# A fifth score buffer, batch 0's routing behind the score loop, expert 0 begun on half its slots, and a low half moved in the ramp

## The chip, the cores and the metric

One core of one Trainium2 chip runs the whole program. The metric is the device time of one execution in microseconds. Five engines work side by side, each on its own instruction stream in its own order: TensorE (PE, matrix products), VectorE (DVE), ScalarE (ACT), GpSimd (POOL) and SyncE (SP, which here only issues DMA transfers, one after the other). They are kept in step by semaphores that the framework sets from the tiles that instructions read and write.

## The reference

Three layers follow each other. Attention has 2 batches of 8 heads, 768 positions and 64 channels; a query sees only the keys whose 6 sign bits (of the product with a random projection) equal its own:

```python
mask = q_bucket[:, :, :, None] == k_bucket[:, :, None, :]
scores = np.where(mask, scale * np.matmul(q, k.transpose(0, 1, 3, 2)), -1000000000.0)
scores = scores - np.max(scores, axis=-1, keepdims=True)
attn = np.exp(scores); attn = attn / (np.sum(attn, axis=-1, keepdims=True) + 1e-09)
x = np.matmul(attn, v)                              # -> 1536 tokens of 512 channels
```

A mixture of 8 experts follows: the softmax of `x @ w_gate` picks one expert for each token and a weight for it; each expert takes at most 384 tokens, in order, and the rest give zero:

```python
h = np.maximum(np.einsum('ecd,edf->ecf', disp, w1), 0.0)   # 512 -> 1024
y = np.einsum('ecf,efd->ecd', h, w2)                       # 1024 -> 512
out[i] = gate_w[i] * y[expert_idx[i], pos[i]]
```

Last is a dense layer, 512 to 2048 to 512: `h = x @ w_in; g = h * np.clip(h + 3.0, 0.0, 6.0) / 6.0; g @ w_out`.

## The kernel before

**Numbers in two halves.** Products that need more precision than one 16-bit pass are made of a high half (a rounded copy) and a low half (what the rounding left). So a value x appears as `hi` and `lo`, `phi` and `plo`, `wh` and `wl`, `xh` and `xl`, `hh` and `hl`; the high half is a copy by ACT or DVE, the low half a subtraction by DVE or POOL, and PE makes three products: high by high, high by low, low by high.

**The score loop.** The 16 heads have 6 blocks of 128 keys each, 96 blocks in all, and `for k in range(STEPS + LAG + 2)` runs over them in steps. In step k the program order is: work that is due by k - 0.5; `high(k-1)`, the cast `phi` of the exponentials `pf` (ACT, or DVE where `on_dve` says so); `scores(k)`, four matmuls and two exponentials by ACT into a tile `pf` (a ring of four buffers with the tag `pf`); `low(k-2)`, the subtraction `plo = pf - phi` (POOL, except that DVE does all but two of the last twelve); `mx(k+8)`, two matmuls into a ring of three PSUM buffers, each followed by a maximum on DVE (the row maxima must be known before a head's scores); at odd k `pv` of two older blocks (36 matmuls); and work that is due by k. Work is put down in a table `later` by `at`, `spread` and `stages` with a step as its time; the table `Q` holds most of these steps. Each engine then executes its own part strictly in this order. `on_dve` reads `Q["hl"]` for the last twelve steps, counted from step 84.

**The operands of a head.** Before a head's maxima can be computed, its q and k must stand in the four tiles X, Y, K1, K2 of `sets[h % 4]`, as high and low halves beside rows of sign bits. `halves` allots the tiles `hi` and `lo` (from head 2 on one buffer each, which the heads use in turn). For head 3 and later, `prep(h)` lets ACT make `hi`, then issues on SP two transfers of sign bits (`put_bits`) and four of `hi` into the set; its second part makes `lo` (DVE, `low_half`, one `scalar_tensor_tensor`) and sends it with two transfers (`send_low`). For head 3 the two parts are due at steps 6 and 7.25. Heads 0 to 2 go through `prep0`: ACT writes the high halves straight into the set, and only `lo` is sent by DMA. In `prep0` the low half of heads 0 and 1 is made by POOL out of a scaled copy `rs`, that of head 2 by DVE, both its parts at step 5 (`at(5.0, run, pre[2])`).

A buffer that is written again must have been read to the end by everything that used it: the `lo` of head 3 goes into the buffer from which the `lo` of head 2 is sent.

**The end of the loop and the transition.** `route(b)` works out, for the tokens of batch b, the expert and the place among its slots (`oh`, `rh`, and `ohr`, six columns of one-hot rows); `weigh(b)` works out the gate's weight (`jg`, `j`, `rg`). For batch 0 both are spread over the last steps of the loop, mostly on DVE. `evac(h)` divides a head's sums by the row sums (three DVE operations that read PSUM; `xp`); for head 14 it is due at step 93.5, for head 15 it stands behind the loop (`scaled`, `columns`). Behind it comes batch 1's routing, then the one-hot products `windows` that give `ids` and `gates`, the gather of expert 0's tokens from memory, their scaling, transposition (`psa`) and split into `xh` and `xl`. `heat(n)` issues n matmuls whose result nobody reads. `high_w` casts a 512-column piece of a weight (ACT), `low_w` makes the low halves of pieces that are cast (DVE), in order, and the number of them that it makes at a call depends on how many are there.

**The experts.** Each expert has 224 slots in two groups of `GW` = 112. `gemm1(e, f)` makes 128 of the 1024 hidden channels: 12 matmuls of 224 columns into one of three PSUM buffers `psh`, then ACT writes `hh` and DVE `hl` from it. `gemm2` follows, then the dense layer, whose output is scattered to memory.

Of the kernel before, what the change touches and what calls it, by code (L numbers as in the profile page):

```python
# [63 lines left out]
def moe_attention_kernel(ctx, tc, qk, v, vt, pj, wg, w1, w2, win, wout, out, cap):  # L64
# [212 lines left out]
    def weigh(b):
# [33 lines left out]
    Q = {'tk': (84, 86), 'v': (-3.25, -4.75, -1.75, -2.25), 'vg': (-6.5, -6.75), 'vgd': 1, 'pr': (-13.0, -12.75, -12.0, -12.5), 'prd': 0.6, 'b0': 7.75, 'b': 1.75, 'bd': 0.5, 'vm0': (9.5, 10.5, 11.5, 12.5), 'vm': (-0.5, 4.75, 7.0, 12.25), 'vs': 13.25, 'pa': 1.5, 'ev': 0.5, 'lvt': -5.0, 'v4': (2.0, 4.25, 10.0, 16.25), 'vg0': (1.85, -4.4, 9.0), 'p2': 3.5, 'lr': (0.25, 1.25, 2.25), 'lv': 4.0, 'vsd': 0.75, 'ac': (1, 1, 2, 4, 6, 7, 8, 10), 'hd': (3, 5, 17), 'hn': (0, 0, 3, 1, 1, 1, 0, 0), 'ap': (0,), 'h0': (7,), 'hl': (6,), 'l0': (), 'll': (1, 3), 'ht': (6, 3, 7, 6, 3, 2)}  # L311
# [4 lines left out]
    with ExitStack() as actx:  # L316
# [346 lines left out]
        def unmatched(r):  # L663
# [10 lines left out]
            m = pt.tile([P, S], F32, tag="pf", name=f"um{r}", bufs=4)  # L674
# [12 lines left out]
            y = pt.tile([P, S], F32, tag="pf", name=f"uy{r}", bufs=4).rearrange("p (c h d) -> p c h d", c=NC, h=2)  # L687
# [33 lines left out]
        def vsplit(h):  # L721
# [17 lines left out]
            if h > 3:  # L739
# [4 lines left out]
        fill = pt.tile([P, S], F32, tag="pf", name="fill", bufs=4)  # L744
# [107 lines left out]
        at(5.0, run, pre[2])  # L852
# [38 lines left out]
        at(STEPS - 2, store, NH // 2 - 1, 0, D)  # L891
# [697 lines left out]
```

## Time and profile before

| | |
|---|---|
| runs | 652.09, 653.40, 652.09 us; median 652.09 |
| the profiled execution | 653.98 us, of which its span is 652.3 us |
| PE busy | 623.4 us (96%), 5530 instructions |
| DVE busy | 478.8 us (73%), 1056 |
| ACT busy | 435.9 us (67%), 882 |
| POOL busy | 234.0 us (36%), 222 |
| score loop | to 218.6 us |
| transition | 218.6 to 232.8 us |
| experts, dense layer, scatter | from 232.8 us |

The span is the time from the first instruction to the last; 1.7 us of the execution lie outside it. All times below are microseconds from the span's start. In a timeline a row is a group of like instructions without a gap: start, length, engine, line of the kernel, operation, result<-operands, how many; in square brackets the engine's idle time just before and what ended it. "DVE L459" there is an instruction of line 459 of the kernel above. In a table of windows each engine has its busy time in the stretch and the number of instructions; PEclk is the clock that TensorE was granted, as a share of the full one.

### The profile page before, as it was taken

The numbers are of one execution on the slowest core, as the hardware profiler recorded it, in microseconds if no ns is written. First come the engines' busy times: TensorE is split into PE (matmuls) and PEld (weight loads), VectorE is DVE, ScalarE is ACT, GpSimd is POOL, SyncE is SP. The second block draws the span as 40 slices with busy tenths as digits, with TensorE's granted clock in tenths as the row PEclk, the third lists the DMA queues.
The fourth block names the chain that finished last, engine by engine and source line by source line (L and its number), as shares of the span: only waits on it lengthen the run. The fifth ranks groups of instructions, "written<-read, shape, count | busy, mean of one in ns | idle before, by whom it ended". The sixth has DMA issues, their size and how long they took to land.

```text
span 652.3 us, 14467 instructions
## 1 busy us (share of the span) xinstructions
PE 623.4 (96%) x5530; PEld 452.5 (69%) x5530; DVE 478.8 (73%) x1056; ACT 435.9 (67%) x882; POOL 234.0 (36%) x222
## 2 busy tenths in 40 slices
PE   8999999999998799999999999999999999999892
PEld 3678788788887589999999985555555555555441
DVE  6889998898999888888988887888887332222410
ACT  8878888788888657677777745554445685555820
POOL 6666978978994142210866100000000020000021
PEclk9999999999999999999999999999999999999997
DMA  6658568656474188877677553444440020000011
GB/s 196 204 137 230 166 159 230 167 132 179 100 203 145 36 286 276 250 248 238 207 241 252 164 170 117 135 129 140 151 131 31 1 81 17 1 1 0 2 50 53
DMA packets 35732, 92.19 MB, mean 141 GB/s; under 512 B 6778, under 2 KB 12250, under 8 KB 35650
## 3 DMA queue, kind: packets, MB, share of 16 engines
q1 hardware_dynamic: 32562, 83.75, 43.2%
q0 software_dynamic: 2400, 7.36, 3.4%
q8 instruction: 46, 0.75, 0.5%
q14 instruction: 36, 0.29, 0.1%
q10 hardware_dynamic: 688, 0.03, 0.1%
HBM read 67.14 MB, written 6.29 MB: 113 GB/s over the span
## 4 chain that ended last, share of the span: by engine, by line
PE 56%; DMA 4%; ACT 3%; issue 1%; DVE 1%; POOL 0%; POOLq 0%; DVEq 0%; ACTq 0%
PE psg L1363 17%; PE pso L1390 15%; PE psy L1141 11%; PE psh L1114 11%; DMA out_dram<-os,inv 3%; ACT junk L1317 2%; PE psa L1091 1%; ACT gh L1373 1%; DVE rl L1366 1%; DMA xg<-xd,ids 1%; DMA xd<-xp 1%; ACT rl L1365 0%; POOL xg L1072 0%; ACT xp L944 0%; POOL out_dram L1405 0%
## 5 line engine op out<-in xcount | busy, mean ns | idle before, releaser
L493 POOL TENSOR_TENSOR plo<-pf,phi 128x768 f16<-128x768 f32 x86 | 145.3, 1713 | 19.7 <-DVE phi L489 10.0
L1405 POOL DMA_INDIRECT out_dram<-os,inv x12 | 12.1, 1012 | 272.6 <-DVE os L1397 244.5
L482 ACT ACTIVATE pf<-pst 128x384 f32<-128x384 f32 x192 | 83.1, 486 | 30.0 <-PE pst L481 25.3
L459 DVE TENSOR_REDUCE mx<-psm 128x1 f32<-128x384 f32 x192 | 96.0, 546 | 6.8 <-PE psm L456 6.6
L164 DVE SCALAR_TENSOR_TENSOR wl<-raw,wh 128x1024 f16<-128x1024 f32 (+1 forms) x68 | 83.4, 1230 | 5.8 <-ACT wh L158 5.1
L1363 PE MATMUL psg<-yTh,ch 128*128 128x512 f16 (+1 forms) x256 | 83.4, 326 | 3.2 <-DVE rl L1366 3.2
L1363 PE MATMUL psg<-yTl,ch 128*128 128x512 f16 (+1 forms) x256 | 83.4, 326 | 0.0
L1363 PE MATMUL psg<-yTh,cl 128*128 128x512 f16 (+1 forms) x256 | 83.4, 326 | 0.0
L1366 DVE SCALAR_TENSOR_TENSOR rl<-rl,psg 128x512 f32<-128x512 f32 x64 | 35.0, 551 | 64.4 <-ACT rl L1365 64.0
L480 PE MATMUL pst<-Y,K 128*128 128x384 f32 x192 | 74.9, 390 | 2.5 <-ACT pf L482 2.5
L1363 PEld LDWEIGHTS <-ch 128*128 128x128 f16 x512 | 50.1, 98 | 35.9
L487 ACT ACTIVATE phi<-pf 128x768 f16<-128x768 f32 x85 | 71.7, 844 | 1.9
L1390 PE MATMUL pso<-ch,gh 128*128 128x512 f16 x192 | 72.8, 379 | 0.0
L1390 PE MATMUL pso<-ch,gl 128*128 128x512 f16 x192 | 72.8, 379 | 0.0
L1390 PE MATMUL pso<-cl,gh 128*128 128x512 f16 x192 | 72.8, 379 | 0.0
L158 ACT ACTIVATE wh<-raw 128x1024 f16<-128x1024 f32 (+1 forms) x68 | 67.4, 998 | 0.5 <-issue 0.5
L1390 PEld LDWEIGHTS <-gh 128*128 128x128 f16 x384 | 37.6, 98 | 42.3
L1141 PE MATMUL psy<-hh,wl 128*128 128x224 f16 x256 | 66.3, 259 | 0.0
L1141 PE MATMUL psy<-hl,wh 128*128 128x224 f16 x256 | 66.3, 259 | 0.0
L1141 PE MATMUL psy<-hh,wh 128*128 128x224 f16 x256 | 66.3, 259 | 0.0
L481 PE MATMUL pst<-X,K 77*128 77x384 f32 x192 | 65.4, 341 | 0.6 <-DMA X<-rm 0.6
L508 PE MATMUL psv<-vh,phi 128*128 128x73 f16 x576 | 64.0, 197 | 0.0
(251 smaller groups left out, 1477.2 us busy)
## 6 DMA issues: line engine op xcount, KB each, us to landing
raw<-in_w_dram SPq DMA_DIRECT2D x64, 512.0 KB
rc<-in_win_dram SPq DMA_DIRECT2D x16, 512.0 KB
rc<-in_wout_dram SPq DMA_DIRECT2D x16, 512.0 KB
r<-in_qk_dram SPq DMA_DIRECT2D x16, 384.0 KB
K<-hi SPq DMA_DIRECT2D x26, 192.0 KB
vr<-in_v_dram SPq DMA_DIRECT2D x4, 768.0 KB
vt<-in_vt_dram SPq DMA_DIRECT2D x8, 384.0 KB
K<-lo SPq DMA_DIRECT2D x16, 192.0 KB
```

The lines of the kernel that those rows point to most:

```text
L158: act.activation(wh[e, i][:, c : c + n], r, AF.Copy, scale=(S1, S2)[i // 2])
L164: dve.scalar_tensor_tensor(out=wl[e, i][:, c : c + n], in0=r, scalar=(S1, S2)[i // 2], in1=wh[e, i][:, c : c + n], op0=ALU.mult, op1=ALU.s ...
L459: dve.tensor_reduce(out=mm[:, c, n : n + 1], in_=ps[:, :HS], axis=AX.X, op=ALU.max)
L480: pe.matmul(ps[:, :HS], st["K1"][:, kc], st["Y"][:, qc], start=True, stop=False)
L481: pe.matmul(ps[:, :HS], st["K2"][0:77, kc], st["X"][0:77, qc], start=False, stop=True)
L482: act.activation(pf[:, qc], ps[:, :HS], AF.Exp, scale=0.125 / SC / SC)
L487: act.activation(phi_t[k], pf_t[k], AF.Copy)
L493: eng.tensor_tensor(out=plo_t[k], in0=pf_t.pop(k), in1=phi_t[k], op=ALU.subtract)
L1114: pe.matmul(ps, l[:, c], r[:, k], start=n == 0, stop=n == 3 * KD - 1)
L1141: pe.matmul(ps, l, r, start=n == 0, stop=n == 3 * KF - 1)
L1363: pe.matmul(ps, l, x, start=n == 0, stop=n == 3 * KD - 1)
L1390: pe.matmul(po[blk][s], l, r, start=first and n == 0, stop=last and n == 2)
```

## The change

Five edits, which touch different places.

1. **The ring `pf`** has five buffers instead of four; every tile with this tag is declared so.
2. **The ramp.** The low half of head 2 is made by POOL, out of a scaled copy that POOL makes too, before the loop (one more `next(pre[2])`). Its two transfers are issued at step 6.5 instead of 5, behind the first part of `prep(3)`, which stays at step 6.
3. **The end of the loop.** `hl` goes from (6,) to (8, 10): of the last steps' casts, DVE makes `phi` 92 and 94 instead of 90. `tk` loses 86, so one small POOL copy goes; another is left out for head 15. Batch 0's `jg` and `j` operations go from DVE to POOL. Its `rg` and its six `ohr` columns come behind the loop, three of the columns by ACT (two activations each). `evac(14)` moves from step 93.5 to 97.5, the store of head 14's half from 94 to 98.
4. **Weight pieces of expert 0.** Of the five `high_w` behind the loop one stays there, one comes behind head 15's `xp`, and four (one of which stood elsewhere) come behind `run(rgen)`; the `low_w(1)` behind the loop goes, and `low_w(2)` moves behind `weigh(1)`. The pieces of low halves that are left for the first `low_w()` of the expert loop are four instead of three.
5. **Expert 0.** `begin(f, i)` issues, for f = 0 and 1, the four matmuls of the first slot group (112 columns) with `wh` (i = 0) and `wl` (i = 1). The first set stands between the two groups' transposes, the others behind the second's. `gemm1` then makes for these f the rest: `wh` by `xl` for the first group, and all three products for the second. The `heat` between the two groups (`HT[4]`) has 2 matmuls instead of 3, and the one behind them (`HT[5]`, 2 matmuls) goes.

```diff
+            if c == n - 1 if b else c < 3:
                 off = rtile([P], "off")
                 act.activation(off, iota_r, AF.Square, bias=place[:, c : c + 1], scale=-1.0)
...
         def prep0(h):
             r, hi, lo = halves(h)
+            x = pt.tile([P, S], F32, tag="pf", name=f"rs{h}", bufs=5)
             if h < 2:
                 act.activation(x, r, AF.Copy, scale=SC)
+            else:
+                pool.tensor_scalar(out=x, in0=r, scalar1=SC, scalar2=None, op0=ALU.mult)
...
-            if h < 2:
-                pool.tensor_tensor(out=lo, in0=x, in1=f32(hi), op=ALU.subtract)
-            else:
-                low_half(lo, r, hi)
+            pool.tensor_tensor(out=lo, in0=x, in1=f32(hi), op=ALU.subtract)
             yield
             send_low(h, lo)
...
         run(pre[1])
+        next(pre[2])
         load_r(4)
...
-        at(5.0, run, pre[2])
+        at(6.5, run, pre[2])
...
-                at(k + Q["ev"], evac, h)
+                at(k + Q["ev"] if h < NH - 2 else 97.5, evac, h)
...
+        r0, w0 = route(0, lambda: misc("psr0")), weigh(0)
+        stages(r0, [66 + 1.5 * i for i in range(8)] + [84.5, 85.25, 87.25, 87.75, 88.25])
+        stages(w0, (84, 86, 87.25, 88.5, 90.5, 91.5))
...
-        for q in range(4):
-            high_w(wp1, 0, 0, 512 * q, 512)
-        high_w(wp1, 0, 1, 0, 512)
-        low_w(1)
+        run(w0)
+        high_w(wp1, 0, 0, 0, 512)
+        run(r0)
         heat(ps_t, "t", HT[0])
...
+    def begin(f, i):
+        if i == 0:
+            begun[f] = ps_h.tile([P, W], F32, tag="h", name=f"psh0{f}")
+        l = (wh, wl)[i][0, 0]
+        for k in range(KD):
+            c = slice(k * 512 + f * P, k * 512 + (f + 1) * P)
+            pe.matmul(
+                begun[f][:, 0:GW], l[:, c], xs_t[0][0][:, k, 0:GW], start=i + k == 0, stop=False, skip_group_check=True
+            )
...
+        todo = [(l, r, 0, W) for l, r in ((a, xh), (b, xh), (a, xl))]
...
+            todo = [(a, xl, 0, GW)] + [(l, r, GW, W) for l, r in ((a, xh), (b, xh), (a, xl))]
...
     run(rgen)
+    for q in range(2, 4):
+        high_w(wp1, 0, 0, 512 * q, 512)
+    for q in range(2):
+        high_w(wp1, 0, 1, 512 * q, 512)
...
-    low_w(2)
     run(wgen)
     windows(ps2, ohr, rg, [B - 1])
     heat(HT[3])
+    low_w(2)
...
     low_w(1)
+    begin(0, 0)
     scale_x(0, 1)
     lows.append(make_x(0, 1))
-    heat(HT[5])
+    begin(0, 1)
+    begin(1, 0)
+    begin(1, 1)
```

What SP issues in the ramp, before (`lo2`, `hi3` and `lo3` are the halves of heads 2 and 3, `b0` the sign bits; the number ahead of a row is its place in the engine's stream):

```order
23 L378 DMA K12_148<-lo2_252 64x768
24 L379 DMA Y2_147<-lo2_252 64x768
25 L415 DMA X3_150<-b0_302 12x768
26 L416 DMA K23_153<-b0_302 12x768
27 L403 DMA X3_150<-hi3_589 64x768
28 L404 DMA K23_153<-hi3_589 64x768
29 L405 DMA K13_152<-hi3_589 64x768
30 L406 DMA Y3_151<-hi3_589 64x768
31 L378 DMA K13_152<-lo3_591 64x768
32 L379 DMA Y3_151<-lo3_591 64x768
```

And in the changed kernel:

```order
23 L415 DMA X3_150<-b0_304 12x768
24 L416 DMA K23_153<-b0_304 12x768
25 L403 DMA X3_150<-hi3_589 64x768
26 L404 DMA K23_153<-hi3_589 64x768
27 L405 DMA K13_152<-hi3_589 64x768
28 L406 DMA Y3_151<-hi3_589 64x768
29 L379 DMA K12_148<-lo2_252 64x768
30 L380 DMA Y2_147<-lo2_252 64x768
31 L379 DMA K13_152<-lo3_591 64x768
32 L380 DMA Y3_151<-lo3_591 64x768
```

The two transfers of `lo2` go from ahead of the sign bits and of `hi3` to behind them, and are now the last ones before those of `lo3`.

What DVE does at the end of the loop, before:

```order
455 L296 TENSOR_TENSOR jg0_4355<-jg0_4355,j20_4357 128x24
456 L297 TENSOR_SCALAR j20_4357<-jg0_4355 128x6x4
457 L489 CAST phi90_4422<-pf90_4342 128x768
458 L493 TENSOR_TENSOR plo90_4424<-pf90_4342,phi90_4422 128x768
459 L273 TENSOR_SCALAR ohr_110<-iota_r_70,pl0_4271 128x128 x2
460 L204 TENSOR_TENSOR rg_109<-oh_103,j20_4357 128x384
461 L493 TENSOR_TENSOR plo91_4440<-pf91_4359,phi91_4411 128x768
462 L273 TENSOR_SCALAR ohr_110<-iota_r_70,pl0_4271 128x128
463 L518 TENSOR_SCALAR rd14_4480<-psv14_4301,sc3_3283 128x6
464 L521 RECIPROCAL rd14_4480<-rd14_4480 128x6
465 L526 TENSOR_TENSOR xp14_4479<-psv14_4301,rd14_4480 128x6x72
466 L659 CAST nflag_164<-psu_4407 1x8
```

And now:

```order
453 L661 TENSOR_REDUCE nflag_164<-nflag_164 1x1
454 L489 CAST phi92_4483<-pf92_4412 128x768
455 L493 TENSOR_TENSOR plo92_4485<-pf92_4412,phi92_4483 128x768
456 L493 TENSOR_TENSOR plo93_4496<-pf93_4423,phi93_4472 128x768
457 L489 CAST phi94_4537<-pf94_4474 128x768
458 L493 TENSOR_TENSOR plo94_4539<-pf94_4474,phi94_4537 128x768
459 L493 TENSOR_TENSOR plo95_4541<-pf95_4487,phi95_4535 128x768
460 L518 TENSOR_SCALAR rd14_4580<-psv14_4301,sc3_3285 128x6
461 L521 RECIPROCAL rd14_4580<-rd14_4580 128x6
462 L526 TENSOR_TENSOR xp14_4579<-psv14_4301,rd14_4580 128x6x72
463 L204 TENSOR_TENSOR rg_109<-oh_103,j20_4355 128x384
464 L273 TENSOR_SCALAR ohr_110<-iota_r_70,pl0_4272 128x128 x3
```

The `jg` and `j` operations and the one-hot columns are gone from between the subtractions, the cast of block 90 with them; the casts of 92 and 94 have come in, and head 14's evacuation (`rd14`, `xp14`) stands behind the last subtraction, followed by `rg` and three one-hot columns.

What DVE does between the last two gather scalings and the first `hl` of expert 0, before:

```order
588 L164 SCALAR_TENSOR_TENSOR wl0_1_4635,wlo_88<-raw0_1_0_4084,wh0_1_4634 128x512
589 L1080 TENSOR_SCALAR xg01_5152<-xg01_5152,gates_78 128x512
590 L1097 SCALAR_TENSOR_TENSOR xl0_5192<-psa00_5193,xh0_5191 128x4x112
591 L1097 SCALAR_TENSOR_TENSOR xl0_5192<-psa01_5204,xh0_5191 128x4x112
592 L164 SCALAR_TENSOR_TENSOR wl0_1_4635,wlo_88<-raw0_1_0_4084,wh0_1_4634 128x512
593 L164 SCALAR_TENSOR_TENSOR wl0_1_4635,wlo_88<-raw0_1_1_4108,wh0_1_4634 128x512 x2
594 L1118 SCALAR_TENSOR_TENSOR hl0_5230<-psh00_5231,hh0_5229 128x224
```

And now:

```order
577 L164 SCALAR_TENSOR_TENSOR wl0_0_4623,wlo_88<-raw0_0_1_4025,wh0_0_4622 128x512
578 L1082 TENSOR_SCALAR xg01_5163<-xg01_5163,gates_78 128x512
579 L1099 SCALAR_TENSOR_TENSOR xl0_5203<-psa00_5204,xh0_5202 128x4x112
580 L1099 SCALAR_TENSOR_TENSOR xl0_5203<-psa01_5219,xh0_5202 128x4x112
581 L164 SCALAR_TENSOR_TENSOR wl0_1_5151,wlo_88<-raw0_1_0_4086,wh0_1_5150 128x512 x2
582 L164 SCALAR_TENSOR_TENSOR wl0_1_5151,wlo_88<-raw0_1_1_4110,wh0_1_5150 128x512 x2
583 L1142 SCALAR_TENSOR_TENSOR hl0_5257<-psh00_5213,hh0_5256 128x224
```

Ahead of `hl0` stood three weight pieces behind the two `xl`; now four stand there.

## Rows read from the trace of the kernel before

**Rows 1.** Windows by stage: busy us per engine with instructions, clock, DMA share, GB/s.

```profile
176.00:203.00 27.00, 26.03 (x340) 21.73 (x336) 25.72 (x60) 22.10 (x42) 23.10 (x18) 1.00 0.60 166
...
203.00:219.00 16.00, 14.22 (x247) 11.65 (x247) 15.32 (x37) 13.98 (x27) 3.62 (x6) 1.00 0.36 106
...
233.00:250.00 17.00, 17.00 (x180) 16.82 (x179) 16.09 (x49) 11.70 (x31) 5.38 (x5) 1.00 0.91 306
...
644.00:652.30 8.30, 0.00 (x0) 0.00 (x0) 0.00 (x0) 0.00 (x0) 0.96 (x1) 0.50 0.09 34
```

**Rows 2.** Timeline of DVE in the ramp: start, duration, engine, line, operation, wait.

```profile
30.21 3.41 DVE L374 SCALAR_TENSOR_TENSOR lo<-r,hi 128x768 fp32r<-128x768 f32 x1
...
34.02 2.40 DVE L459 TENSOR_REDUCE mx<-psm 128x1 f32<-128x384 f32 x5
...
37.43 0.96 DVE L374 SCALAR_TENSOR_TENSOR lo<-r,hi 128x768 fp32r<-128x768 f32 x1 [1.00 <-DMA Y<-lo]
...
42.06 0.62 DVE L419 TENSOR_SCALAR b<-psb,pj_sb 128x384 fp32r<-128x384 f32 x1 [0.61 <-PE psb L430]
```

**Rows 3.** Timeline of POOL in the ramp.

```profile
29.55 3.25 POOL L493 TENSOR_TENSOR plo<-pf,phi 128x768 f16<-128x768 f32 x2
```

**Rows 4.** Timeline of SP in the ramp: its DMA issues, same columns.

```profile
33.65 0.55 SPq L378 DMA_DIRECT2D K<-lo  x1
...
36.62 0.52 SPq L403 DMA_DIRECT2D X<-hi  x1
...
40.75 0.71 SPq L379 DMA_DIRECT2D Y<-lo  x1
```

**Rows 5.** Windows at the ramp's transfers (DMA share: second number from the end).

```profile
42.00:43.00 1.00, 1.00 (x7) 0.91 (x7) 0.94 (x2) 0.39 (x1) 1.00 (x2) 1.00 1.07 267
...
43.00:44.00 1.00, 1.00 (x9) 0.34 (x9) 0.93 (x4) 1.00 (x4) 1.00 (x2) 1.00 0.64 141
...
44.00:45.00 1.00, 1.00 (x6) 0.82 (x6) 1.00 (x4) 1.00 (x3) 1.00 (x1) 1.00 0.00 0
```

**Rows 6.** Timeline of ACT in the ramp.

```profile
31.80 0.87 ACT L482 ACTIVATE pf<-pst 128x384 f32<-128x384 f32 x2 [1.61 <-PE pst L481]
...
33.66 0.84 ACT L370 ACTIVATE hi<-r 128x768 fp32r<-128x768 f32 x1 [0.98 <-DVE vh L738]
```

**Rows 7.** Timeline of PE at steps 9 and 10.

```profile
39.43 0.51 PE L456 MATMUL psm<-K,X 76*128 76x384 f32 x2
...
41.90 0.44 PE L480 MATMUL pst<-Y,K 128*128 128x384 f32 x1
```

**Rows 8.** Timeline of ACT in the loop's last fifth.

```profile
177.59 0.87 ACT L482 ACTIVATE pf<-pst 128x384 f32<-128x384 f32 x2 [1.24 <-POOL vh L741]
...
207.99 0.87 ACT L482 ACTIVATE pf<-pst 128x384 f32<-128x384 f32 x2 [1.70 <-POOL plo L493]
...
215.43 0.84 ACT L487 ACTIVATE phi<-pf 128x768 f16<-128x768 f32 x1
```

**Rows 9.** Timeline of DVE at the loop's end.

```profile
206.20 1.81 DVE L273 TENSOR_SCALAR ohr<-iota_r,pl 128x128 f16<-128x128 f16 x2
...
213.41 0.61 DVE L526 TENSOR_TENSOR xp<-psv,rd 128x432 f32<-128x432 f32 x1
...
214.20 3.67 DVE L493 TENSOR_TENSOR plo<-pf,phi 128x768 f16<-128x768 f32 x4
...
218.81 0.23 DVE L518 TENSOR_SCALAR rd<-psv,sc 128x6 f32<-128x6 f32 x1 [0.34 <-PE psv L510]
```

**Rows 10.** Timeline of POOL at the loop's end.

```profile
206.29 1.66 POOL L493 TENSOR_TENSOR plo<-pf,phi 128x768 f16<-128x768 f32 x1
```

**Rows 11.** Timeline of PE at expert 0's first gemm.

```profile
232.82 0.54 PE L1114 MATMUL psh<-xh,wh 128*128 128x224 f16 x4 [0.20 <-ACT xh L1094]
```

**Rows 12.** Timeline of DVE at expert 0's first gemm.

```profile
234.56 1.09 DVE L164 SCALAR_TENSOR_TENSOR wl<-raw,wh 128x512 f16<-128x512 f32 x1
...
235.58 0.38 DVE L1118 SCALAR_TENSOR_TENSOR hl<-psh,hh 128x224 f16<-128x224 f32 x1
```

More of the change, by code (lines that the diff above doesn't have):

```diff
@@ L267, in route @@
                 yield
-            if b and c == n - 1:
+            if c == n - 1 if b else c < 3:
                 off = rtile([P], "off")
@@ L291, in weigh @@
         jt = rtile([n, NW], f"jg{b}")
-        dve.tensor_tensor(out=jt, in0=jo[:, b], in1=bc(gt[:, b], NW), op=ALU.mult)
+        eng = dve if b else pool
+        eng.tensor_tensor(out=jt, in0=jo[:, b], in1=bc(gt[:, b], NW), op=ALU.mult)
         j2 = rtile([n, 2 * NW], f"j2{b}", F16)
-        dve.tensor_copy(j2[:, :, 0:NW], jt)
+        eng.tensor_copy(j2[:, :, 0:NW], jt)
         yield
-        dve.tensor_tensor(out=jt, in0=jt, in1=j2[:, :, 0:NW], op=ALU.subtract)
-        dve.tensor_scalar(out=j2[:, :, NW:], in0=jt, scalar1=LS, scalar2=None, op0=ALU.mult)
+        eng.tensor_tensor(out=jt, in0=jt, in1=j2[:, :, 0:NW], op=ALU.subtract)
+        eng.tensor_scalar(out=j2[:, :, NW:], in0=jt, scalar1=LS, scalar2=None, op0=ALU.mult)
         yield
@@ L366, in halves @@
             if h == 1:
-                hi = pt.tile([P, S], F32, tag="pf", name=f"hi{h}", bufs=4).bitcast(F32R)
+                hi = pt.tile([P, S], F32, tag="pf", name=f"hi{h}", bufs=5).bitcast(F32R)
             else:
@@ L673, in unmatched @@
                 sp.dma_start(out=x, in_=rows)
-            m = pt.tile([P, S], F32, tag="pf", name=f"um{r}", bufs=4)
+            m = pt.tile([P, S], F32, tag="pf", name=f"um{r}", bufs=5)
             ps = misc(f"psu{r}")
@@ L738, in vsplit @@
             dve.memset(t[:, :, DE:VA], 1.0)
-            if h > 3:
+            if 3 < h < NH - 1:
                 c = t[:, :, VA + o : VA + o + 1]
                 pool.tensor_copy(c, c)
-        fill = pt.tile([P, S], F32, tag="pf", name="fill", bufs=4)
+        fill = pt.tile([P, S], F32, tag="pf", name="fill", bufs=5)
         neg, zrow = fill[0:1], fill[32:33]
@@ L890, in moe_attention_kernel @@
             at(STEPS - 8 + i, load_w, 0, 2, i)
-        at(STEPS - 2, store, NH // 2 - 1, 0, D)
+        at(STEPS + 2, store, NH // 2 - 1, 0, D)
         def due(k):
@@ L946, in moe_attention_kernel @@
                 store(h // 2, D, P, slice(c - 2, c + 1))
+        high_w(wp1, 0, 0, 512, 512)
         rgen = route(1, lambda: misc("psr2"))
@@ L1101, in make_x @@
         return low
+    begun = {}
+    def begin(f, i):
[7 more added lines that the diff above has]
+            )
     def gemm1(e, f):
@@ L1108, in gemm1 @@
         a, b = wh[e, f // 4], wl[e, f // 4]
-        ps = ps_h.tile([P, W], F32, tag="h", name=f"psh{e}{f}")
-        n = 0
-        for l, r in ((a, xh), (b, xh), (a, xl)):
+        todo = [(l, r, 0, W) for l, r in ((a, xh), (b, xh), (a, xl))]
+        ps = None
+        if e == 0:
+            ps = begun.pop(f, None)
+        if ps is None:
+            ps = ps_h.tile([P, W], F32, tag="h", name=f"psh{e}{f}")
+        else:
+            todo = [(a, xl, 0, GW)] + [(l, r, GW, W) for l, r in ((a, xh), (b, xh), (a, xl))]
+        n = KD * len(todo)
+        for l, r, u, v in todo:
             for k in range(KD):
+                n -= 1
                 c = slice(k * 512 + (f % 4) * P, k * 512 + (f % 4 + 1) * P)
-                pe.matmul(ps, l[:, c], r[:, k], start=n == 0, stop=n == 3 * KD - 1)
-                n += 1
+                pe.matmul(
+                    ps[:, u:v], l[:, c], r[:, k, u:v], start=u == 0 and v == W and r is xh and l is a and k == 0,
+                    stop=n == 0, skip_group_check=v - u < W,
+                )
         i = e * KF + f
```

12 lines of the change are left out of this document (4 added, 8 removed).

## The prediction

> **What bounds the kernel now.** I read the windows by stage first, then the timelines at the places that the five edits touch, engine by engine, and on them only what stands in square brackets: who was waited for. In the score loop (to 218.6) two engines are nearly full. From 176 to 203 DVE is busy for 25.72 of 27 us and PE for 26.03; in the loop's last 16 us it is DVE with 15.32, against 14.22 for PE and 13.98 for ACT [rows 1]. So a wait that DVE or PE gets early in the loop is not made good later, and work taken from DVE at the loop's end is worth its own time until ACT becomes the bound. From 233 on PE is full (17.00 of 17, [rows 1]): there only matmul time and what delays the first gemms count. The transition between them is a chain (routing of batch 1, store, gather, transposes) that the change leaves in its order; it moves as a whole with the loop's end, and I cost it at 0: what is added to it (weight pieces on ACT and DVE) stands where these engines wait for the gather.
>
> **The ramp: where the change costs.** `lo` has one buffer. `lo3` is written into it by DVE and has to wait until both transfers of `lo2` have read it. Before, the trace shows this wait: `lo3` starts at 37.43 after 1.00 of idle time that ended with DMA Y<-lo [rows 2]. The first of the pair was issued at 33.65 and took 0.55 to issue [rows 4], so the second went out at about 34.2 and the pair was through 3.2 later.
>
> What the edit takes away: DVE's `lo2`, 3.41 us at 30.21, since POOL subtracted beside it (29.55, two in 3.25 [rows 3]); the same operation took 0.96 at 37.43 [rows 2]. ACT's `hi3` waited 0.98 for it [rows 6], because `lo2` reads the single `hi` buffer. That wait goes: `pf` at 31.80 ends at 32.67, `hi3` runs to about 33.5. The two POOL operations that make `lo2` instead stand ahead of the loop, where POOL waits for a scale; 0.
>
> What it adds: on SP the pair `lo2` now stands behind four transfers of `hi3`, and these can't go before `hi3` is there, at 33.5. Before, the same four and a pair behind them (that of `lo3`) were issued from 36.62 to 40.75 [rows 4], 4.13 us for the start of the last. The DMA engines were full with them (1.07 from 42 to 43, 0.64 from 43 to 44, nothing from 44 to 45 [rows 5]): data moved until about 43.6, that is 7.0 from the first issue. By this row the new pair is through at 33.5 + 7.0 = 40.5; with a notice that comes 1 later (44.6 is the latest that the empty window allows, taking the notice as up to 1 behind the data), at 41.5. The low end is 33.5 + 4.13 + 3.2 - 1.2 = 39.6: pace of the issues as before without the slowest one's excess of 1.2 over the others (estimate), and the pair's 3.2 behind its second issue. I take L = 41.2, near the row that shows six transfers in this order, against 37.43 before.
>
> The Trainium skill bears on this in "DMA: Bandwidth & Descriptors", section "Queues, rings and completion order": on each DMA engine the descriptors of one issuing sequencer's ring are consumed in the order of the ring. By that, `lo2` can't overtake `hi3`, and L would lie at the upper part of my bounds; if it could overtake, at 37 or so and no wait would be left. Rows 5 agree with a full queue, but no row shows the order inside it.
>
> Who waits for that: behind `lo3` on DVE stand the maxima of `mx(16)`; PE has three PSUM buffers for them, `mx(16)` takes two, the first of `mx(17)` the third, and the second of `mx(17)` needs the first maximum to be done. That is L + 0.96 [rows 2] + 0.48 (five maxima in 2.40 [rows 2]). Behind it in PE's order stand `pv` of two blocks and then `scores(10)`. Before, the second `mx(17)` started at about 39.6 (the pair of 39.43 [rows 7]) and `scores(10)` at 41.90 [rows 7], 2.3 later. So now `scores(10)` comes at L + 0.96 + 0.48 + 2.3 = L + 3.74 = 44.94, which is 3.04 late. With L of 39.6 it is 1.4, with 41.9 it is 3.7. Everything behind is fed by `scores`, and the one idle time of DVE that could take some of it up, 0.61 at 42.06 [rows 2], waits for PE and moves with it. The 1.0 that PE gains earlier, since the maxima come sooner, ends at this wait. Term: **+3.0** (1.4 to 3.7).
>
> **The fifth buffer.** ACT waited for POOL before it could write `pf`: 1.24 at 177.59 [rows 8] and three shorter ones between 157 and 186, 2.3 in all as the upper bound of the gain. But DVE is full in that stretch [rows 1], and ACT isn't; an ACT that runs ahead gives DVE nothing to do sooner than it can. At the least the gain is 0. I take **-0.3**, by the small gap that DVE has there.
>
> **The end of the loop.** From DVE's stream go six one-hot columns (1.81 for two at 206.20, beside POOL's subtraction at 206.29 [rows 9, 10]; the others a quarter to 0.4 each; 2.5 in all), `jg` and `j` (about 0.6), `rg` (0.5), head 14's evacuation (three operations, of which `xp` at 213.41 is the longest, 0.61 [rows 9]; 1.0) and a cast (0.6): 5.2. Two casts come in, 1.1. DVE alone would end its last subtraction 4.1 sooner than at 217.87 (four of them in 3.67 from 214.20 [rows 9]), at 213.8. ACT sets a limit close by: its last cast began at 215.43 and lasted 0.84; its wait of 1.70 for POOL at 207.99 [rows 8] goes with the fifth buffer, and one cast of 0.75 goes to DVE, so it ends at 216.27 - 1.70 - 0.75 = 213.8. The last subtraction (0.92) is behind that cast: 214.8, or up to 215.5 if POOL's subtraction slows DVE elsewhere as it did at 206.20. Before, `scaled` of head 15 began at 218.81 [rows 9], 0.94 after the last subtraction, for the last `pv`. Now DVE has 1.0 for the evacuation, 0.5 for `rg` and three columns (0.6) in front of it: 2.1, longer than `pv`. So `scaled` is at 216.9 to 217.6. Term: **-1.4** (-1.0 to -1.9): of the 4.1 us moved, DVE's new tail and ACT keep the rest.
>
> **Expert 0.** Four matmuls of 224 columns took 0.54 at 232.82 [rows 11], of which ends overlap; over the stretch it is 180 matmuls in 17.00 us [rows 1], 0.094 each. Behind the last `xh` PE has for f = 0 and 1 32 matmuls of 112 columns, at half of that 1.5, instead of 24 with 2.3: about -0.7. But DVE has four weight pieces ahead of `hl0` instead of three. A piece takes 0.61, and 1.09 at 234.56 beside POOL; `hl0` ran at 235.58 [rows 12], 2.8 after the first gemm's start. PE has three `psh` buffers, so f = 3 waits for `hl0`, which comes 0.6 later against a PE that is 0.7 ahead, and f = 4 for `hl1`, with a larger piece between. PE therefore stops where it did not before (17.00 of 17 [rows 1]). Bounds: -0.7 (nothing waits) and +0.7 (a piece at 1.09 and one more behind it). I take **+0.4**, by the row at 234.56, where two such pieces stood already.
>
> **Sum.** 3.0 - 0.3 - 1.4 + 0.4 = +1.7. The profiled execution took 653.98, span 652.3 and 1.7 around it, and lies 1.89 above the median 652.09. So 655.7 for an execution like that one, and 653.8 for the median.
>
> **Rivals.**
> *The transfers are not late.* If the DMA engines take the six faster when nothing else is queued and the pair is through by 37.5, 4 us from the first issue, `lo3` waits no longer than before, and DVE and ACT keep the 1.0 that they gain from the missing `lo2`. The point from which it decides is L = 41.90 - 3.74 = 38.2: below that the ramp gains. For it: the lone pair needed 3.2. Against it: six transfers in a full queue needed 7.0 [rows 4, 5]. Time: -0.3 - 1.4 + 0.4 - 0.5 = -1.8, 650.3: faster.
> *The wait is short, or the later terms are larger.* L at 39.6 (+1.4), or the fifth buffer worth 1.5 instead of 0.3: the sum is about 0, 652.1. For it: bounds above; against it: the full DMA windows and the full DVE.
> *The clock falls.* In the new gap PE has little to do from about 38.4 to 43, which before it never had in the loop. After the last matmul the granted clock is 0.50 [rows 1], the lower of the two levels (1.2 GHz). If that happens in the gap, some 3 us of PE work behind it take twice as long, of which the idle shares around it take half: +1.5, 655.3. Against it: the gap is short beside the 8 us of that row. The Trainium skill ("TensorE: Matmul & The Clock Gate", section "What's actually happening") says that an idle engine goes to half the clock and returns after sustained work; by it this rival would hold if the gap were long enough, and the trace shows only the end of the program.
>
> **How the numbers follow.** Forecast 0.46 (its own range 652.7 to 655.0), clock 0.12, short wait 0.20, transfers not late 0.22. A measurement tells 0.2%, 1.3 us, from no change: 650.8 and 653.4 are the marks. Of the forecast three quarters lie above 653.4 (0.34) and the clock's 0.12 with it: slower 0.46. The short wait gives 0.18 and the forecast's lower part 0.12 to the same: 0.30. The rest, 0.24, is faster. The range goes from 650.1 to 655.8.
>
> **What would show it.** In the trace after: DVE's `lo` at step 7 behind an idle time of some 6 us that ends with DMA Y<-lo, at 41 instead of 37.4; PE idle ahead of a lone `psm` at 42 to 43; `scores(10)` at 45; no ACT wait for POOL at the loop's end; `scaled` of head 15 1.4 sooner relative to step 10; `hl0` later and an idle PE before `psh` 3 or 4. I am wrong if `lo3` starts before 38.2, if the lateness that `scores(10)` shows is not there any more at step 84, or if the loop's end gives over 2.

## The result, and the profile after

| | before | after |
|---|---|---|
| median of 6 runs | 652.75 us | 657.91 us |
| their range | 651.42 to 655.37 | 657.30 to 658.55 |
| profiled execution (span) | 653.98 (652.3) | 657.34 (655.6) |
| PE, DVE, ACT, POOL busy | 623.4, 478.8, 435.9, 234.0 | 623.2, 475.3, 436.8, 240.6 |

The ratio is 1.0083, with an interval from 1.0064 to 1.0101: slower by 0.8%, some 5 us, where 1.7 was forecast; 657.91 lies above the forecast's range, which ended at 655.8. PE and DVE, the two fullest engines, have no more work than before (POOL has 6.6 more, ACT 0.9); the time is in waits.

**The ramp.** DVE of the changed kernel (columns as in [rows 2]); these rows answer to the two of `lo` there:

```profile
33.64 1.95 DVE L459 TENSOR_REDUCE mx<-psm 128x1 f32<-128x384 f32 x4 [0.26 <-PE psm L456]
...
41.68 0.96 DVE L375 SCALAR_TENSOR_TENSOR lo<-r,hi 128x768 fp32r<-128x768 f32 x1 [6.09 <-DMA K<-lo]
...
47.26 0.62 DVE L419 TENSOR_SCALAR b<-psb,pj_sb 128x384 fp32r<-128x384 f32 x1 [1.55 <-PE psb L430]
```

The subtraction of `lo2` at 30.21 is gone, and `lo3` starts at 41.68 after 6.09 of idle time that a transfer of `lo` ended (it was 1.00 before, and the start 37.43). SP's issues, to be read beside [rows 4]:

```profile
33.51 0.52 SPq L403 DMA_DIRECT2D X<-hi  x1
...
36.05 0.68 SPq L379 DMA_DIRECT2D K<-lo  x1
...
36.77 1.69 SPq L380 DMA_DIRECT2D Y<-lo  x1
...
42.67 0.46 SPq L379 DMA_DIRECT2D K<-lo  x1
```

The first transfer of `hi3` goes out at 33.51, the pair `lo2` at 36.05 and 36.77, behind the four of `hi3`. PE, beside [rows 7]: the two `psm` of `mx(17)`, which stood together before, then `scores(10)`:

```profile
38.61 0.34 PE L456 MATMUL psm<-K,X 76*128 76x384 f32 x1
...
43.16 0.44 PE L456 MATMUL psm<-K,X 76*128 76x384 f32 x1 [4.22 <-DVE mx L459]
...
47.09 0.44 PE L480 MATMUL pst<-Y,K 128*128 128x384 f32 x1
```

PE waits 4.22 for the maximum that stands behind `lo3`. From the second `psm` (43.16) to `scores(10)` it takes 3.93; before it was 2.3. The windows show what goes with it (the first number after the engines' columns is the clock):

```profile
40.00:42.00 2.00, 0.00 (x0) 0.00 (x0) 0.32 (x1) 0.26 (x1) 0.00 (x0) 1.00 0.05 14
...
42.00:44.00 2.00, 0.83 (x13) 0.74 (x14) 2.00 (x4) 0.00 (x0) 0.00 (x0) 0.91 0.11 26
...
44.00:46.00 2.00, 2.00 (x33) 1.75 (x34) 1.67 (x5) 0.00 (x0) 1.29 (x1) 0.50 0.65 171
...
46.00:48.00 2.00, 2.00 (x14) 0.82 (x6) 0.74 (x2) 0.19 (x1) 2.00 (x3) 0.74 0.00 0
```

PE did nothing from 40 to 42, and from 44 to 46 its granted clock is 0.50, the 1.2 GHz level; from 46 to 48 it is 0.74 on average. In windows of 0.25 us the clock is still 1.00 up to 43.5, 0.50 from 43.75 to 47.0 and 1.00 again from 47.25: it fell when PE, idle from 38.95 to 43.16, had just begun again, so that the work behind the gap pays for it.

**The loop's end.** DVE, ACT and PE at the last blocks:

```profile
208.36 1.70 DVE L204 TENSOR_TENSOR rh<-oh,jt 128x192 f16<-128x192 f16 x1
...
219.46 0.96 DVE L493 TENSOR_TENSOR plo<-pf,phi 128x768 f16<-128x768 f32 x1 [0.46 <-ACT phi L487]
...
220.82 0.61 DVE L526 TENSOR_TENSOR xp<-psv,rd 128x432 f32<-128x432 f32 x1
...
222.75 0.23 DVE L518 TENSOR_SCALAR rd<-psv,sc 128x6 f32<-128x6 f32 x1 [0.34 <-DVEq L933]
...
208.17 1.67 POOL L493 TENSOR_TENSOR plo<-pf,phi 128x768 f16<-128x768 f32 x1
...
214.41 0.88 ACT L482 ACTIVATE pf<-pst 128x384 f32<-128x384 f32 x2 [0.32 <-PE pst L481]
...
216.48 0.87 ACT L482 ACTIVATE pf<-pst 128x384 f32<-128x384 f32 x2 [0.31 <-PE pst L481]
...
217.68 0.88 ACT L482 ACTIVATE pf<-pst 128x384 f32<-128x384 f32 x2 [0.33 <-PE pst L481]
...
218.59 0.84 ACT L487 ACTIVATE phi<-pf 128x768 f16<-128x768 f32 x1
...
213.76 0.44 PE L480 MATMUL pst<-Y,K 128*128 128x384 f32 x1 [0.23 <-ACT pf L482]
...
217.02 0.44 PE L480 MATMUL pst<-Y,K 128*128 128x384 f32 x1 [0.22 <-ACT pf L482]
```

DVE's last subtraction (219.46) waits 0.46 for the last cast; ACT waits 0.31 for PE there, and PE 0.22 for ACT, so these two go round with each other; two steps of PE, from one of the `pst` rows to the other, take 3.26. `scaled` of head 15 (222.75) comes 2.3 behind the end of the last subtraction, after the evacuation, `rg`, three columns and 0.34 of DVE's own queue at the branch. `rh` took 1.70 beside a POOL subtraction (208.17). Before, that subtraction stood beside two one-hot columns [rows 9, 10], and `rh` was short:

```profile
204.02 0.36 DVE L204 TENSOR_TENSOR rh<-oh,jt 128x192 f16<-128x192 f16 x1
```

**Expert 0.** PE's first gemms and DVE's rows ahead of `hl0`, beside [rows 11, 12], and the window from the second `xh` to the first `psy`, now and (last row) before:

```profile
239.77 0.54 PE L1136 MATMUL psh<-xh,wh 128*128 128x224 f16 x4 [0.80 <-DVE sum L972]
...
241.25 0.54 PE L1136 MATMUL psh<-xh,wh 128*128 128x224 f16 x4 [0.17 <-DVE hl L1142]
...
237.71 1.09 DVE L164 SCALAR_TENSOR_TENSOR wl<-raw,wh 128x512 f16<-128x512 f32 x1
...
238.73 0.68 DVE L164 SCALAR_TENSOR_TENSOR wl<-raw,wh 128x512 f16<-128x512 f32 x1
...
239.34 0.38 DVE L1142 SCALAR_TENSOR_TENSOR hl<-psh,hh 128x224 f16<-128x224 f32 x1
...
235.37:245.85 10.48, 9.40 (x119) 8.96 (x115) 9.84 (x34) 7.42 (x21) 6.40 (x5) 1.00 0.88 296
...
232.23:242.09 9.86, 9.66 (x100) 9.34 (x99) 9.12 (x31) 7.41 (x21) 4.57 (x4) 1.00 0.92 292
```

PE is busy for 9.40 of 10.48 us now, where it was for 9.66 of 9.86; the two waits make 0.97. The wait of 0.80 is put down to a short memset that stands right behind `hl0` on DVE; the buffer that PE waits for is freed by `hl0`, at 239.34 to 239.72, behind the fourth weight piece.

How late each mark is against the profiled execution of before, in us (marks: the reciprocal of a head's evacuation, the second `xh`, the first `psy`, the span). The kernels e1 to e4, e6 and e9 are told below:

| mark (before) | after | e2 | e1 | e3 | e4 | e6 | e9 |
|---|---|---|---|---|---|---|---|
| head 0 (43.30) | 5.20 | 4.79 | -0.83 | -0.87 | 2.93 | -1.25 | -1.02 |
| head 6 (116.25) | 5.11 | 4.57 | -0.99 | -1.03 | 3.50 | -1.48 | -1.23 |
| head 7 (130.16) | 4.41 | 3.90 | -1.60 | -1.71 | 3.13 | -2.17 | -1.91 |
| head 13 (202.12) | 4.24 | 3.78 | -1.74 | -1.66 | 3.03 | -2.33 | -2.02 |
| head 15 (219.07) | 3.93 | 3.78 | -2.03 | -1.98 | 2.74 | -2.61 | -2.64 |
| xh (232.23) | 3.14 | 3.07 | -2.54 | -2.36 | 2.11 | -3.35 | -3.46 |
| psy (242.09) | 3.76 | 3.08 | -1.92 | -1.72 | 2.73 | -2.73 | -3.45 |
| span (652.3) | 3.3 | 1.9 | -2.2 | -1.8 | 2.1 | -3.9 | -4.2 |

All columns drop by 0.6 to 0.7 between heads 6 and 7 (e4 by 0.4) and by 0.4 to 0.8 between head 15 and `xh`, e2's too, which has nothing of the change there. So that is no gain of theirs. At the first place the one profiled execution of before lost it: its trace shows PE waiting for the row of maxima, which ACT and the rest then wait for.

```profile
120.43 0.44 PE L481 MATMUL pst<-X,K 77*128 77x384 f32 x1 [0.41 <-DMA X<-rm]
```

At the second place kernels with the same code there differ among themselves: from head 15 to `xh` the kernel before takes 13.16, e2 12.45 and e8 13.92.

### The profile page after: what moved, and what is told of

The parts are those of the page before. It is cut to its first block, busy times and chain, and to the rows that moved or that the text cites. A ratio compares the mean times of both kernels' runs of the same rounds, so it can differ in the third digit from the quotient of the medians.

```text
span 655.6 us, 14512 instructions
## 1 busy us (share of the span) xinstructions
PE 623.2 (95%) x5551; PEld 453.0 (69%) x5551; DVE 475.3 (73%) x1049; ACT 436.8 (67%) x887; POOL 240.6 (37%) x226
## 4 chain that ended last, share of the span: by engine, by line
PE 55%; DMA 3%; ACT 3%; issue 2%; DVE 2%; POOL 0%; POOLq 0%; DVEq 0%; ACTq 0%
PE psg L1393 17%; PE pso L1420 15%; PE psy L1165 11%; PE psh L1136 11%; DMA out_dram<-os,inv 3%; ACT junk L1347 2%; PE psa L1093 1%; ACT gh L1403 1%; DVE rl L1396 1%; DMA xg<-xd,ids 1%; DVE wl L164 0%; ACT rl L1395 0%; DMA xd<-xp 0%; ACT xp L945 0%; ACT xh L1096 0%
```

## The experiments

Each was timed in 5 rounds beside the kernel before; ratios are to it, with their intervals of 95%.

**e1: `lo2` sent at step 5 again.**

```diff
-        at(6.5, run, pre[2])
+        at(5.0, run, pre[2])
```

> The changed kernel, with one edit: the two transfers of lo2 are issued at step 5 again, ahead of hi3; POOL still makes lo2. Theory (the single lo buffer: lo3 waits for lo2's transfers, which wait behind hi3, and the clock falls in the gap): the idle time of 6.09 before lo3 and the one of 4.22 on PE go, scores(10) comes at about 41 instead of 47.09, and the time falls by 5 to 6.5, to about 652. Rival (POOL's two added operations in the ramp, or the fifth buffer, delay the ramp): scores(10) stays at 46 or later and the time above 656. Rival (SP's order is not decisive, since the transfers of lo2 take long anyway): lo3 still starts after 39 and the time falls by less than 3.

Measured: 651.79 us, ratio 0.9990 (0.9976 to 1.0004), 6.1 below the changed kernel. DVE:

```profile
35.49 1.62 DVE L375 SCALAR_TENSOR_TENSOR lo<-r,hi 128x768 fp32r<-128x768 f32 x1
```

`lo3` starts at 35.49 without a wait, although POOL still makes `lo2` and `pf` has five buffers. That one line carries the whole loss.

**e2: the kernel before with the ramp's edit alone** (POOL's two operations, `next(pre[2])`, `at(6.5, ...)`; diff as above).

> The kernel before, with the ramp's edit alone (POOL makes lo2, its transfers at step 6.5). Theory: the whole loss is in it, so 652.75 + 5.2 = 658, with lo3 at 41.7 and the granted clock at half from 44 to 47. Rival (the other edits cost as well): clearly below 657.

Measured: 656.48 us, ratio 1.0068 (1.0043 to 1.0093), so 4.0 slower than the kernel before (652.52 beside it). That is under the 5.2 expected, with an interval that holds it (2.8 to 6.1); it is under the rival's mark of 657 too, but not clearly, so a small cost of the other edits is not ruled out by this run alone (e1 rules out a large one). `lo3` at 41.27 after 5.92 of idle time:

```profile
41.27 0.96 DVE L374 SCALAR_TENSOR_TENSOR lo<-r,hi 128x768 fp32r<-128x768 f32 x1 [5.92 <-DMA K<-lo]
...
44.00:46.00 2.00, 2.00 (x30) 1.34 (x27) 1.26 (x4) 0.00 (x0) 1.70 (x2) 0.50 0.45 128
```

The wait and the half clock are both there without any of the other edits.

**e3: two buffers for `lo`.**

```diff
-        return r, hi, ph.tile([P, S], F32R, tag="lo", name=f"lo{h}")
+        return r, hi, ph.tile([P, S], F32R, tag="lo", name=f"lo{h}", bufs=2)
```

> The changed kernel with two buffers for lo instead of one, nothing else; SP issues in the same order. Theory: lo3 has nothing to wait for but hi3 and starts at about 35.7 when its maxima are done; no idle time on DVE or PE, no fall of the clock; 651 to 652.5. Rival (the late transfers of lo2 or hi3 themselves hold up head 2's or head 3's scores, not the buffer): the ramp is still late by over 2 at scores(10), and the time above 654.

Measured: 652.58 us, ratio 1.0006 (0.9990 to 1.0022). The pair still goes out behind `hi3`, and nobody minds:

```profile
36.01 0.69 SPq L379 DMA_DIRECT2D K<-lo  x1
...
36.74 1.68 SPq L380 DMA_DIRECT2D Y<-lo  x1
...
35.47 1.53 DVE L375 SCALAR_TENSOR_TENSOR lo<-r,hi 128x768 fp32r<-128x768 f32 x1
```

`lo3` starts before the pair `lo2` is even issued. So it is the shared buffer that makes the order on SP costly, not the lateness of `lo2` for its readers.

**e4: idle matmuls in PE's gap.**

```diff
                 ps = ps_m.tile([P, 512], F32, tag="m", name=f"psm{h}{c}{n}")
+                if (h, c, n) == (2, 5, 1):
+                    heat(ps_v, "v", 18)
```

> The changed kernel with 18 matmuls that nobody reads ahead of the second mx(17) of PE, in the gap of 4.22 us. The wait stays: lo3 at 41.7. Theory that 1.6 to 2 of the 5.2 are the clock that falls in the gap: it stays at 1.00 from 42 to 48, scores(10) comes 3.7 to 3.9 after lo3 (45.5 instead of 47.09), and the time falls by 1.5 to 2, to 656. Rival (the clock's fall is hidden, since DVE sets the pace behind the gap): the time stays within 0.5 of 657.9.

Measured: 657.23 us, ratio 1.0073 (1.0050 to 1.0096). By time alone it can't be told from the changed kernel, as the intervals lie over each other. By the trace it can:

```profile
40.95 0.96 DVE L375 SCALAR_TENSOR_TENSOR lo<-r,hi 128x768 fp32r<-128x768 f32 x1 [5.90 <-DMA K<-lo]
...
38.25 2.33 PE L336 MATMUL heatv<-idle_sb 128*128 128x512 f16 x10
...
42.43 0.44 PE L458 MATMUL psm<-K,X 76*128 76x384 f32 x1
...
44.82 0.44 PE L482 MATMUL pst<-Y,K 128*128 128x384 f32 x1
...
44.00:46.00 2.00, 2.00 (x19) 1.19 (x15) 1.95 (x6) 0.46 (x2) 2.00 (x2) 1.00 0.30 97
```

The clock stays at 1.00, and from `lo3` to `scores(10)` it is 3.87 (40.95 to 44.82) instead of 5.41 (41.68 to 47.09). The fall of the clock is worth 1.5 at this place. How much of it reaches the end is not shown: the forecast of 656 was missed, the median is only 0.7 below the changed kernel's, between theory and rival, and the profiled execution, whose span is 1.2 shorter, took 656.14 and is one of the two fastest of six. By the table e4 is 2.3 ahead of the changed kernel at head 0 (0.7 of it since `lo3` starts sooner), and 1.2 at head 13.

**e5: e1, with head 14's evacuation and store back at 93.5 and 94.**

```diff
-                at(k + Q["ev"] if h < NH - 2 else 97.5, evac, h)
+                at(k + Q["ev"], evac, h)
-        at(STEPS + 2, store, NH // 2 - 1, 0, D)
+        at(STEPS - 2, store, NH // 2 - 1, 0, D)
```

> The changed kernel with lo2 sent at step 5 (as in e1) and with head 14's evacuation and store back at steps 93.5 and 94. In the changed kernel's trace the last subtraction ends at 220.4 and scaled of head 15 begins 2.41 later, behind the evacuation (1.0), rg and three columns (1.05) and the branch (0.34). Theory (this tail on DVE, not PE, decides there): the time from the last subtraction to the reciprocal of head 15 falls from 2.66 to about 1.7, the last subtraction comes 0.4 to 0.6 later, since DVE idles only 0.65 in its last six operations, and head 15 is 0.3 to 0.6 earlier than in e1: 651.4. Rival (DVE has no room in the loop's last steps): the last subtraction comes 1.0 later and nothing is gained.

Measured: 652.19 us, ratio 0.9986 (0.9969 to 1.0003): no gain. From head 13's reciprocal to head 15's it is 17.31 (199.56 to 216.87), where e1 takes 16.66 (200.38 to 217.04), and the reason is one that neither the theory nor the rival had:

```profile
209.24 0.23 DVE L518 TENSOR_SCALAR rd<-psv,sc 128x6 f32<-128x6 f32 x1 [1.47 <-PE psv L510]
```

At this place DVE is ahead of PE and stands 1.47 before the evacuation, since head 14's last `pv` isn't done. In the trace moving the evacuation is worth 0.65 once DVE has less to do; in the time e5 can't be told from e1.

**e6: e1 without `begin`** (the four `begin` calls taken out, `heat(3)` behind the transposes).

> The changed kernel with lo2 sent at step 5 and without begin: expert 0's f = 0 and 1 are made whole by gemm1, and three idle matmuls stand behind the transposes. Four weight pieces stay ahead of hl0 on DVE. Theory (the fourth piece, not the half matmuls, sets expert 0's first gemms): from the second xh to the first psy 10.5 us as in e1, so that begin is worth nothing; time as e1, 651.8, within 0.5. Rival (begin itself gains its 0.7 or loses by its many short matmuls): 10.5 changes by over 0.4 in either direction.

Measured: 650.33 us, ratio 0.9956 (0.9941 to 0.9972). From the second `xh` to the first `psy` 10.48, as in e1 (10.48; before and e2: 9.86 and 9.87): as expected, `begin` gains and loses nothing there. But the time is 1.5 below e1, which was not expected. Ahead of the dense layer's last product the profiled e6 is only 0.46 ahead of e1 (638.01 and 638.47 for its end); the rest of what the profiles differ by lies in the chain of the last six scatters, each of which waits for the one before. Its first and last in e1, then in e6:

```profile
622.32 0.96 POOL L1435 DMA_INDIRECT out_dram<-os,inv  x1 [85.02 <-DVE os L1427]
...
642.89 0.96 POOL L1435 DMA_INDIRECT out_dram<-os,inv  x1 [2.52 <-DMA out_dram<-os,inv]
```

```profile
621.85 0.96 POOL L1432 DMA_INDIRECT out_dram<-os,inv  x1 [84.71 <-DVE os L1424]
...
640.67 0.96 POOL L1432 DMA_INDIRECT out_dram<-os,inv  x1 [3.58 <-DMA out_dram<-os,inv]
```

That is 20.57 and 18.82; in the other kernels' profiles it lies between 18.8 and 20.6 too (before 20.59, after 20.33, e8 18.84).

**e7: e1, with three weight pieces ahead of `hl0`.**

```diff
-    low_w(2)
+    low_w(3)
     ps2 = ps2[:, : 2 * NW * E].rearrange("p (e j) -> p e j", e=E)
```

> The changed kernel with lo2 sent at step 5 and with one weight piece more made ahead of the gates (low_w(3) for low_w(2)), so that three stand ahead of hl0 as before. Theory: from the second xh to the first psy 9.9 instead of 10.5, since hl0 comes 0.6 sooner and the waits of 0.80 and 0.17 on PE shrink; the piece costs at most 0.1 in the transition, where DVE waited 0.50 for the gather: 651.2. Rival (the piece delays the gates and the gather's scaling by its 0.61): nothing gained.

Measured: 651.72 us, ratio 0.9986 (0.9966 to 1.0005). From `xh` to `psy` 9.88 (229.83 to 239.71): the 0.6 is won in the trace, and PE's wait of 0.80 is 0.20:

```profile
233.63 0.54 PE L1136 MATMUL psh<-xh,wh 128*128 128x224 f16 x4 [0.20 <-DVE sum L972]
```

In the time it is too small to be told from e1. With `begin`'s half matmuls in place, it is the time of before (9.86) and no better.

**e8: the kernel before with five buffers for `pf`** (each `bufs=4` of the tag made 5).

> The kernel before with five buffers for pf instead of four and nothing else. Theory (ACT's waits for POOL between 157 and 186 give nothing back, and the 0.7 by which the changed kernel's profile was less late at head 7 than at head 6 was a late transfer X<-rm in the one profiled execution of before): 652.5 as before, within 0.5; head 7 to head 13 take as long as in the kernel with the ramp alone, 71.84. Rival (the fifth buffer gave the 0.7): the time from head 7 to head 13 falls below 71.5 or the whole by over 0.7.

Measured: 652.16 us, ratio 0.9988 (0.9969 to 1.0007): nothing that can be measured. From head 7 to head 13 it takes 72.11, e2 with four buffers 71.84.

**e9: the version that the runs point to.** e1 without `begin`, with `low_w(3)`, and

```diff
-        spots(rg[:, b], oh[:, b], j2)
+        spots(rg[:, b], oh[:, b], j2, dve if b else pool)
...
-            dve.tensor_scalar(
+            (dve if b else pool).tensor_scalar(
                 out=ohr[:, b, c], in0=iota_r, scalar1=place[:, c : c + 1], scalar2=None, op0=ALU.is_equal
```

with the first three columns on POOL in steps 93 to 95 and `rg` at 92.5.

> The version that the runs point to: the changed kernel with lo2 sent at step 5, without begin, with three weight pieces ahead of hl0, and with batch 0's rg and three of its one-hot columns on POOL in steps 92 to 95, where POOL idled for 8.5 us. Theory: DVE's tail behind the last subtraction falls from 2.41 to 1.4 (evacuation 1.0, branch 0.34), head 15's reciprocal 1.0 sooner than in e6 relative to head 13; the three pieces give 0.5 more ahead of psy: 648.9 to 649.5. Rival (POOL beside DVE's subtractions slows these by as much): no gain over e6, 650.3.

Measured: 649.93 us, ratio 0.9964 (0.9949 to 0.9979), the only version beside e6 whose interval lies below 1, but not measurably faster than e6 and short of the forecast. From `xh` to `psy` 9.87, as forecast. At the loop's end head 15 gains 0.34 on e6 (16.33 from head 13's reciprocal to its own, against 16.67), not 1.0:

```profile
208.14 5.53 POOL L273 TENSOR_SCALAR ohr<-iota_r,pl 128x128 f16<-128x128 f16 x3
...
216.18 0.22 DVE L518 TENSOR_SCALAR rd<-psv,sc 128x6 f32<-128x6 f32 x1 [0.93 <-DVEq L933]
```

POOL takes 1.85 on average for a column for which DVE takes 0.2, and DVE now waits 0.93 in its queue at the branch instead of 0.34; why it waits longer is not shown.

**e10: the changed kernel without `begin`.**

> The changed kernel as it is (lo2 sent at step 6.5), without begin and with three idle matmuls in its place. Without begin e6 was 1.5 below e1 in the median, though from the second xh to the first psy both took 10.48; the profiled e6 was 1.75 shorter in the chain of the last six scatters alone. Theory A (that is chance of the scatter's landing in either kernel): the time is within 0.6 of 657.9. Theory B (begin costs 1.5 somewhere that these marks don't show): 656.4. The ramp's lateness stays as in the changed kernel: lo3 at 41.7.

Measured: 657.72 us, ratio 1.0078 (1.0062 to 1.0095), against 1.0083 of the changed kernel; `lo3` starts at 41.41. In the changed kernel, then, `begin` costs nothing that can be measured, as theory A has it. For the 1.5 between e1 and e6 this settles less. In the profiles it goes with the scatter chain, but a chain whose length were chance in each execution would hardly part two sets of 12 runs (e1 650.83 to 653.09, e6 649.77 to 651.03). With the pair sent at step 5, both kernels without `begin` (e6, and e9 with its other edits: ratios 0.9956 and 0.9964) lie below the three with it (e1, e5, e7: 0.9990, 0.9986, 0.9986). Whether `begin` has a price there, or the scatters land differently for some other reason, stays open.

## Why the prediction was wrong

The direction was right and the size was not: +1.7 was forecast, and the measured loss is three times that. By the prediction's own steps:

- **The wait of `lo3`: right.** L was taken as 41.2 and is 41.68; the second `mx(17)` came 1.48 behind it, 1.44 was worked out; the queue order on SP and the single buffer are shown by e1 and e3. The rival that the transfers aren't late (0.22) is refuted: six transfers took 8.2 from the first issue to the end of the wait (33.51 to 41.68), where the forecast's 7.0 and 1 for the notice make 8.0. The DMA share is 0.89 on average from 34.5 to 40.0, and 0.00 from 41.0 to the wait's end.
- **From there to `scores(10)`: the term that failed.** It was priced with the 2.3 of before, and took 3.93. The step was mis-sized because the clock was put up as a rival, with a chance of 0.12, instead of as a part of the forecast: in all three traces with this wait and nothing put into the gap (the changed kernel, e2, e10) PE stands idle for 4.22, 4.06 and 3.97, and the granted clock goes to 0.50. Its price, +1.5, agrees with the 1.54 that e4's trace gives back at this place; it isn't a fixed one (in e10 `scores(10)` is 5.77 behind `lo3`, in the changed kernel 5.41), and that the whole of it reaches the end is not shown. The argument against it, that the gap is short beside the 8 us of [rows 1], was no argument, since that row doesn't show how short a gap may be. The Trainium skill says in "TensorE: Matmul & The Clock Gate", section "What's actually happening", that the low clock is the default, which activity releases; the windows after agree, with 0.50 behind an idle stretch of 4.22. With L and the clock the ramp is +5.1 (`scores(10)` at 47.09 instead of 41.90, less 0.1 by which the trace starts later) instead of +3.0. The clock alone would have made the forecast 655.3, still 2.6 too low.
- **The fifth buffer: -0.3 was forecast, and e8 shows nothing** (72.11 against 71.84 from head 7 to head 13).
- **The loop's end: -1.4 was forecast, and it is -0.3** (lateness 4.24 at head 13, 3.93 at head 15; in e1 -1.74 and -2.03). The last subtraction ends at 220.4, that is 14.1 after head 13's reciprocal instead of 15.75: 1.7 sooner, not 3.0. Two bounds were used for it, and both were too early. ACT's last cast ends 13.07 after that reciprocal (219.43), where the forecast had 11.7 and before 14.15: PE was left out, for which ACT waits 0.96 in three waits there, while PE in its last blocks needs 3.26 for two steps (`pst` at 213.76 and 217.02), for matmuls all but 0.22 of it. In e1, e5 and e9 this cast ends 13.06 to 13.09 after the reciprocal too, whatever DVE does meanwhile; no run makes PE shorter there, so that PE sets it is read from the waits. And DVE's own work up to the last subtraction fell by 2.2 (busy 13.13 instead of 15.37), not by the 4.1 that were added up: the two columns' 1.81 beside a POOL subtraction were counted as won, but now `rh` stands beside that subtraction and takes 1.70 instead of 0.36. The tail behind the last subtraction was put at 2.1 and took 2.3, the branch's 0.34 being left out. Of the 1.7, this tail gives back all but 0.3.
- **Expert 0: +0.4 was forecast and it is +0.62** (from `xh` to `psy` 10.48 instead of 9.86), by the fourth weight piece as said; e7 takes it away, e6 shows that `begin` gains nothing there.
- **The base.** The sum by the steps as measured is 5.1 - 0.3 + 0.6 = 5.4, and the medians differ by 5.2. The two profiled executions differ by 3.4, since that of before was slow by some 1.2 against its median of 652.75, and by 0.6 that of the changed kernel fast. The forecast's base was the median of three runs, 652.09; with six it is 652.75, so 0.7 of the miss in the time itself is no term's.

The signs of the terms were right, but for the fifth buffer, which is nothing, and the sum was wrong by the clock (1.5), by the loop's end (1.1), and by 0.5 each for L and for the two small terms.

## What to carry to other kernels

When a transfer is put later in an in-order queue, look for who writes its source buffer next: the price is set by that writer's wait, and here a second buffer took it away within the noise (e3). Where a forecast puts a gap like this one (4.2 us) into TensorE's stream, the fall of the clock behind it belongs into the sum, not among the rivals. A stretch in which three engines are over 85% busy has a bound from each of the three. And an operation that is slow because of its neighbour on another engine gives its excess back only if nothing else takes its place beside that neighbour.

## What the runs showed of the hardware

- Behind an idle stretch of 4.2 us on PE (to 43.16) the granted clock was 0.50 from 43.75 to 47.0 (e2: 0.50 from 44 to 46 too); 18 idle matmuls of 512 columns in the gap held it at 1.00 (e4).
- Six transfers of 64x768 f32, begun within 3.3 us on SP, were through 8.2 after the first issue, and the pair issued last 4.9 after its second issue, where a pair with nothing ahead of it took 3.2. The Trainium skill's rule that a ring's descriptors are consumed in its order ("DMA: Bandwidth & Descriptors", section "Queues, rings and completion order") agrees with that; the trace doesn't show the order itself, since engines as full as these (a share of 0.89 from 34.5 to 40) would delay the pair in any order.
- A one-hot column of 128x128 (`tensor_scalar`, f16) took 1.85 on average on POOL beside DVE's work (e9), and 0.20 on DVE.
- A DVE `tensor_tensor` of 128x192 f16 (`rh`) took 1.70 beside a POOL subtraction of 1.67, and 0.36 without one.
- The chain of the last six scatters took between 18.8 and 20.6 in the profiles of kernels that are alike there.
